# Where the last heads are normalised and split, and when the squares of w1 and w3 are issued, in a fused attention and gated feed-forward kernel

## The chip, the cores and the metric

The kernel runs on one core of a Trainium2 chip. Its engines are TensorE (PE in the profile, with its weight loads as PEld), VectorE (DVE), ScalarE (ACT), GpSimd (POOL) and SyncE (SP), which here only issues transfers between on-chip memory (SBUF) and DRAM. Each engine works off its own queue in order and waits in that queue for what its next instruction needs. The metric is the time of one execution on the device, in microseconds.

## The reference

For x of 2048 tokens by 512 channels:

```python
xn = _layernorm(x)
s = attention(xn, wqkv, wo)        # 32 heads of 16, causal, window of 256 keys, scale 1/4
g = _silu(((_silu(xn @ w1) * (xn @ w3)) @ w2))     # 512 -> 1792 -> 512
return x + s * g
```

In the attention, scores outside the window are set to -1e9 before the softmax. wqkv, wo, w1, w2 and w3 are drawn at run time and multiplied by 8, so the kernel has to find their magnitude itself.

## The kernel before

**Numbers.** Every matrix product but the scores' mask and the values is done in 16-bit pieces: an operand is scaled by a power of two and split into a high part (its cast to fp16) and a low part (what the cast left out), and three products are summed: high by high, high by low, low by high. A split is two instructions, a cast and a subtraction. It is done by ScalarE and GpSimd (the helper `halves`, line 340, runs an elementwise operation on two halves of 256 columns; all its users appear under L340) or by ScalarE and VectorE.

**Tiling.** The tokens are worked through in four tiles t of 512. In each, the 32 heads make four groups g of eight, and a group two units p of four heads; there are 16 pairs (t, g) and 32 units. Attention takes two passes over the scores of a unit. `pass1` computes them to find each row's maximum on VectorE (L662, L676); `pass2` computes them again with the keys on the partitions (L742), adds the masks (L749, VectorE), takes the exponential (L752, ScalarE) and multiplies by the values (L770). The values carry a column of ones, so the denominators come out of the same matmuls.

**From heads to the operand of the output projection.** When a unit's values are done, `finish` (inside `pass2`) moves them to SBUF (`os`), to the tile `on` of the group (eight heads by 16 channels on 128 partitions, 512 tokens) and the denominators to a DRAM tile `dd`. After the second unit, `normalise(t, g)` runs:

- it loads the denominators as a 128 by 32 tile `dr` (L807);
- `invert`, 12 steps later: reciprocal (L812) and scale (L813) on VectorE, a store to the DRAM tile `de` (L815), eight broadcasting loads into `rb` (L819), and on GpSimd the product of `on` and `rb` in two halves (L340). The VectorE part stands inside `issue_after(lasts["emptied"])`, which ties it behind the latest instruction that emptied a PSUM bank;
- `cut`, 26 steps later: GpSimd casts `on` to the high part (L826, two halves) and subtracts for the low part (L340, two halves). The result `O[t, g]` is an operand of `total`.

A step is one piece of work of the program that is written next; `later(n, f)` runs f after n more of them.

**Feed-forward.** `gate_up` (L1013) multiplies by w1 and w3, and L1028, L1032, L1037 and L1046 form and split the product of silu and up; `down` (L1238) multiplies by w2. From t = 2 on the down projection is folded: seven products instead of eight (L1156), whose banks are emptied by L1174, and which `unfold` (L1190) adds up, on VectorE in the last tile. `total` then takes tanh of the result (L1284, ScalarE; a tie to the last exponential stands there too), finishes the silu (L1285), runs the output projection (L1290, 12 matmuls for each of the row blocks b), evicts (L1294), adds x (L1296) and stores. For the last tile this runs for b = 1, 3, 0, and `total_by_columns` does b = 2 in two halves of 256 columns (L1312 to L1323).

**Weights in the first tile.** w1, w3 and w2 are loaded in float32 during t = 0 only (L849 for w1 and w3), measured, split and stored to DRAM in fp16 for the later tiles. To measure means: the sum of squares of each piece (`squares`), a cast of the sums (L262), a matmul with ones that adds them over the partitions (L281 or L286), and a chain of small VectorE instructions that makes a power of two (`powers`). `squares` puts the first `on_act` pieces on ScalarE (L250) and the others on VectorE (L252). `measure(f)` asks for four pieces, two of them on ScalarE for f = 0 and 2, all four afterwards; the weights of q, k and v use `squares` too, with two on ScalarE. Squares of w2 have an instruction of their own in `measure_down`.

**What sets the order.** TensorE's order is the order in which the program is written. The queues of the other engines and of SyncE are put in order by a scheduler that goes by priorities (`urgent` raises one) and by operands, and that obeys `issue_after`: the instruction is put behind the named one in its queue. `behind_exp()` is such a tie, to the latest exponential (L752) issued so far, if there is one.

PSUM, where matmuls write, has two banks m0 and m1 that `bank` hands out in turn to all dense products, two pairs of banks for scores and one pair (po) for the values.

Of the kernel before, what the change touches and what calls it, by code (L numbers as in the profile page):

```python
# [14 lines left out]
AF = mybir.ActivationFunctionType  # L15
# [68 lines left out]
def tile_block(ctx: ExitStack, tc: tile.TileContext, x, wqkv, wo, w1, w3, w2, out):  # L84
    nc = tc.nc
# [27 lines left out]
    def take(dtype):  # L113
        free.sort()
        slot = free.pop(0)[2]
        made = fpool.tile([P, 512 if dtype == F32 else 1024], dtype, name=slot, tag=slot, bufs=1)
        held[id(made)] = slot, made
        return made
# [25 lines left out]
    def later(n, f):  # L144
        made_so_far[0] += 1
        queue.append((now[0] + n, made_so_far[0], f))
# [85 lines left out]
    def behind_exp():  # L232

        return tc.issue_after(lasts["exp"].ins) if "exp" in lasts else nullcontext()
# [5 lines left out]
    def squares(parts, on_act=0, apart=0):  # L240


        ssq = small.tile([P, len(parts)], F32, name="ssq")

        def one(i, raw):

            sq = ppool.tile([P, D], BF16, name="sqa" if i < on_act else "junk", bufs=1)
            if i < on_act:
                with behind_exp():
                    nc.scalar.activation(sq, raw, AF.Square, accum_out=ssq[:, i:i + 1])  # L250
            else:
                nc.vector.tensor_tensor_reduce(out=sq, in0=raw, in1=raw, scale=1.0, scalar=0.0,  # L252
                                               op0=ALU.mult, op1=ALU.add, accum_out=ssq[:, i:i + 1])
        for i, raw in enumerate(parts):
            if apart:
                later(apart * (i + 1), lambda i=i, raw=raw: one(i, raw))
            else:
                one(i, raw)
        sb = small.tile([P, len(parts)], BF16, name="sb")

        def cast():
            lasts["cast"] = nc.vector.tensor_copy(sb, ssq)  # L262
        def behind_bank():

            with tc.issue_after(lasts["emptied"].ins) if "emptied" in lasts else nullcontext():
                cast()
        if apart:
            later(apart * (len(parts) + 1) + 1, behind_bank)
        else:
            cast()  # L270
        return sb
# [65 lines left out]
    def halves(op, out, a, b):  # L337

        for c in (slice(0, 256), slice(256, 512)):
            op(out[:, c], a[:, c], b[:, c])  # L340
# [81 lines left out]
    lasts = {}  # L422
# [298 lines left out]
    def pass2(t, g, p):  # L721
# [54 lines left out]
        def finish():  # L776
            os = opool.tile([P, TW], F32, name="os", bufs=1)
            po = cell["po"]

            def rest():  # L780

                c = slice(0 if t else 64, TW)

                with urgent(), tc.issue_after(lasts["emptied"].ins):
                    nc.vector.tensor_copy(os, po[:, 0, :])
                    nc.vector.tensor_add(os[:, c], os[:, c], po[:, 1, c])
                if p == 0:
                    ON[t, g] = (opool.tile([P, TW], F32, name="on", bufs=1), dpool.tile([8, TW], F32, name="dd"))
                on, dd = ON[t, g]
                for i in range(4):  # L790
                    h = (i // 2) * 4 + 2 * p + i % 2
                    nc.sync.dma_start(on[16 * h:16 * h + 16, :], os[32 * i:32 * i + 16, :])
                nc.sync.dma_start(dd[4 * p:4 * p + 4, :], os[DH::32, :])
                if p == 1:
                    normalise(t, g)
            later(1, rest)
# [6 lines left out]

    def normalise(t, g):
        on, dd = ON.pop((t, g))
        dr = small.tile([P, 32], F32, name="dr")
        nc.sync.dma_start(dr, dd.rearrange("h (b c) -> (h b) c", c=32))  # L807
        rb = opool.tile([P, TW], F32, name="rb", bufs=1)

        def invert():  # L810
            with tc.issue_after(lasts["emptied"].ins):
                nc.vector.reciprocal(dr, dr)  # L812
                nc.vector.tensor_scalar(dr, dr, sc["o"], None, op0=ALU.mult)  # L813
            de = dpool.tile([8, TW], F32, name="de")
            nc.sync.dma_start(de.rearrange("h (b c) -> (h b) c", c=32), dr)  # L815
            for i in range(8):
                p, r, a = i // 4, i // 2 % 2, i % 2
                h = r * 4 + 2 * p + a
                nc.sync.dma_start(rb[16 * h:16 * h + 16, :], de[i:i + 1, :].to_broadcast([16, TW]))  # L819
            halves(nc.gpsimd.tensor_mul, on, on, rb)  # L820

        def cut():
            OT[t, g] = made = take(F16)
            O[t, g] = o = made.rearrange("p (a q) -> p a q", a=2)
            for c in (slice(0, 256), slice(256, 512)):
                nc.gpsimd.tensor_copy(o[:, 0, c], on[:, c])  # L826
            halves(nc.gpsimd.tensor_sub, o[:, 1, :], on, o[:, 0, :])
        later(12, invert)
        later(26, cut)

# [553 lines left out]
    tiles = [(t, g) for t in range(NT) for g in range(NG)]  # L1386
# [190 lines left out]
    for n in range(len(units)):  # L1577
        t = n // 8
# [69 lines left out]
```

## Time and profile before

| | us |
|---|---|
| median of 3 runs | 824.89 |
| lowest and highest of them | 822.91, 829.77 |
| the profiled execution, whole | 824.23 |
| its span in the trace | 822.3 |
| VectorE, ScalarE, GpSimd busy in the span | 632.8, 393.9, 374.3 |

The span runs from the first recorded instruction to the last; the profiled execution's own time has 1.9 us around it. All times in the trace count from the span's start. PE is TensorE, PEld its weight loads, DVE VectorE, ACT ScalarE, POOL GpSimd, SPq, DVEq and so on the engines' sequencers. A line such as L340 is a line of the kernel before; rows name the operation as out<-in with the program's tile names, where `slot` is any of the 55 tiles that are reused for everything without a name of its own, m a bank of the dense products and s a pair of banks of scores.

Three views are used in the prediction. In the page's groups and in the waits, a row gives busy time, count and the idle time ahead, with what ended it. In the chain of waits a row is a start time, a duration and what was on the path then; "issue" is time without any visible wait. In the timeline a row is a start time, how long the row's instructions took together, the engine, line, operation and shapes, the count (x), and in square brackets the idle time just ahead and what ended it. A window row gives start and end, length, the busy time and instruction count of PE, PEld, DVE, ACT and POOL, the granted TensorE clock as a share of full speed, the share of DMA engines busy and GB/s.

### The profile page before, as it was taken

What the parts mean: (1) busy time and instruction counts of PE and PEld (TensorE: products, weight loads), DVE (VectorE), ACT (ScalarE), POOL (GpSimd) and SP (SyncE); (2) the same over time, 40 slices, a digit from 0 to 9 for tenths busy, and PEclk for the clock granted to TensorE, in tenths of its full rate; (3) what the DMA queues carried; (4) which work ended last, traced back from release to release, by engine and by line L of the source; (5) the groups of instructions that cost most, each with busy time, mean ns of one, the idle gap of its engine ahead of it and who ended that gap; (6) DMA issues with size and microseconds to landing.
All of it is one profiled execution on the core that took longest, in us unless ns stands there. A gap on an engine that the chain in (4) does not pass through costs nothing.

```text
span 822.3 us, 23929 instructions
## 1 busy us (share of the span) xinstructions
PE 797.6 (97%) x9176; PEld 404.8 (49%) x9176; DVE 632.8 (77%) x2032; ACT 393.9 (48%) x594; POOL 374.3 (46%) x660
## 2 busy tenths in 40 slices
PE   8997989999999999999999999999999999999995
PEld 4433444444445444444445444466545744466472
DVE  8787688788888767887988887777677877874454
ACT  6879576563546544344443444344444243444410
POOL 2236366232329447155262546330446374831833
PEclk9999999999999999999999999999999999999998
DMA  9979664665743486747555453745543662244311
GB/s 283 256 239 301 220 204 151 209 201 151 211 138 92 144 251 197 215 123 219 159 147 173 122 154 89 203 139 165 171 119 107 169 195 70 62 140 143 123 47 53
DMA packets 109923, 134.71 MB, mean 164 GB/s; under 512 B 18736, under 2 KB 64752, under 8 KB 109808
## 3 DMA queue, kind: packets, MB, share of 16 engines
q1 hardware_dynamic: 109520, 132.66, 54.6%
q8 instruction: 72, 1.18, 0.6%
q10 hardware_dynamic: 288, 0.52, 0.2%
q14 instruction: 43, 0.35, 0.1%
HBM read 91.75 MB, written 37.09 MB: 157 GB/s over the span
## 4 chain that ended last, share of the span: by engine, by line
PE 73%; DVE 10%; DMA 5%; POOL 3%; issue 3%; ACT 3%; SPq 2%; DVEq 0%; POOLq 0%; ACTq 0%
PE m L1013 27%; PE po L770 8%; PE m L1156 7%; PE m L1238 6%; PE m L594 6%; PE s L742 5%; PE m L1290 4%; PE m L564 4%; DVE junk L676 3%; PE s L662 2%; POOL slot L340 2%; DMA slot<-in_B_w_dram 2%; PE po L662 1%; DVE s L749 1%; PE m L1508 1%
## 5 line engine op out<-in xcount | busy, mean ns | idle before, releaser
L1013 PE MATMUL m<-XH,slot 128*128 128x512 f16 x896 | 267.3, 380 | 2.3 <-DVE slot L615 1.0
L752 ACT ACTIVATE pt<-s,es 128x1024 f32<-128x1024 f32 x152 | 167.5, 1112 | 191.1 <-DVE s L749 185.1
L340 POOL TENSOR_TENSOR slot<-slot,slot 128x256 f16<-128x256 f32 (+1 forms) x178 | 117.7, 689 | 204.3 <-ACT slot L1046 80.8
L1013 PEld LDWEIGHTS <-slot 128*128 128x128 f16 x1344 | 124.8, 98 | 156.7 <-issue 13.2
L1013 PE MATMUL m<-XL,slot 128*128 128x512 f16 x448 | 169.8, 379 | 0.0
L749 DVE TENSOR_TENSOR s<-s,MK 128x256 f32<-128x256 f32 (+2 forms) x280 | 118.8, 435 | 52.5 <-PE s L742 47.9
L676 DVE CUSTOM_DVE_ANT_0 junk<-s,MW 128x320 bf16<-128x320 f32 x276 | 134.0, 485 | 17.5 <-PE s L662 11.0
L676 DVE CUSTOM_DVE_ANT_0 junk<-po,MW 128x320 bf16<-128x320 f32 x172 | 83.5, 485 | 4.3
L1238 PE MATMUL m<-slot,slot 128*128 128x512 f16 x336 | 79.2, 380 | 2.5 <-POOL slot L340 2.1
L770 PE MATMUL po<-pt,V 64*32 64x320 f32 (+4 forms) x2880 | 77.2, 342 | 0.7 <-DVE pp L305 0.7
L594 PE MATMUL m<-XH,slot 128*128 128x512 f16 x240 | 70.9, 380 | 1.5 <-DVE slot L1032 0.7
L1156 PE MATMUL m<-slot,slot 128*128 128x256 f16 x588 | 68.4, 273 | 0.0
L1071 POOL TENSOR_TENSOR slot<-slot,slot 128x256 f16<-128x256 f32 x98 | 64.6, 670 | 1.2
L1028 ACT ACTIVATE slot<-m,sgs 128x512 f32<-128x512 f32 x56 | 38.2, 683 | 55.6 <-PE m L1013 50.3
L1156 PEld LDWEIGHTS <-slot 128*128 128x128 f16 x588 | 56.2, 98 | 11.4 <-issue 2.8
L770 PEld LDWEIGHTS po<-pt,V 64*32 64x32 f32 x2880 | 50.5, 106 | 22.8 <-issue 0.8
L1032 DVE SCALAR_TENSOR_TENSOR slot<-slot,m 128x512 f32<-128x512 f32 x56 | 38.3, 684 | 28.1 <-ACT slot L1028 28.1
L742 PE MATMUL s<-qa,KA 50*64 50x320 f16 (+3 forms) x1472 | 58.4, 259 | 0.2 <-DMA qa<-dm 0.2
L594 PEld LDWEIGHTS <-slot 128*128 128x128 f16 x384 | 35.7, 98 | 44.6 <-issue 3.2
L340 POOL TENSOR_TENSOR on<-on,rb 128x256 f32<-128x256 f32 x32 | 26.3, 842 | 64.9 <-DMA rb<-de 42.6
L742 PEld LDWEIGHTS <-KA 50*64 50x64 f16 x1472 | 30.2, 105 | 52.0 <-issue 29.9
L1238 PEld LDWEIGHTS <-slot 128*128 128x128 f16 x336 | 30.7, 98 | 41.4 <-issue 7.5
(186 smaller groups left out, 1125.2 us busy)
## 6 DMA issues: line engine op xcount, KB each, us to landing
slot<-dW SPq DMA_DIRECT2D x98, 256.0 KB
slot<-in_B_w_dram SPq DMA_DIRECT2D x56, 256.0 KB
slot<-dFold SPq DMA_DIRECT2D x48, 256.0 KB
dW<-slot SPq DMA_DIRECT2D x42, 256.0 KB
slot<-in_A_x_dram SPq DMA_DIRECT2D x30, 256.0 KB
KA<-dK SPq DMA_DIRECT2D x24, 288.0 KB
qa<-dQ SPq DMA_DIRECT2D x32, 192.0 KB
slot<-dWQ SPq DMA_DIRECT2D x24, 256.0 KB
```

The source lines that it names most:

```text
L340: op(out[:, c], a[:, c], b[:, c])
L594: nc.tensor.matmul(cell["pp"], w[:, (a * NC + c) * P:(a * NC + c + 1) * P], b[:, c, :], start=(c, i) == parts[0][0], stop=(c, i) == parts[ ...
L676: lasts["maximum"] = nc.vector.tensor_tensor_reduce(out=junk[:, :n], in0=s[:, r, :n], in1=mask, scale=1.0, scalar=NEG, op0=ALU.add, op1=AL ...
L742: nc.tensor.matmul(s[64 * h:64 * h + 64, r, o:o + 64 * n], ka[rows, 2 * p + a, 64 * (m + 4):64 * (m + 5)], qa[rows, 2 * p + a, 64 * (m + k ...
L749: nc.vector.tensor_add(v, v, MK[:, kind, of:of + n, :].unsqueeze(1).to_broadcast([P, 2 * len(which), n, 64]))
L752: lasts["exp"] = nc.scalar.activation(pt, s, AF.Exp, scale=es)
L770: nc.tensor.matmul(cell["po"][32 * i:32 * i + 32, h, 64 * (m + k):64 * (m + k + n)], V[64 * h:64 * h + 64, (4 * t + m // 2) % VB, hd * VW: ...
L1013: nc.tensor.matmul(cell[k], w[:, (a * NC + c) * P:(a * NC + c + 1) * P], b[:, c, :], start=c == 0 and i == 0, stop=c == NC - 1 and i == 2)
L1032: lasts["emptied"] = nc.vector.scalar_tensor_tensor(sg, sg, 1.0, cell[0], op0=ALU.add, op1=ALU.mult)
L1071: nc.gpsimd.tensor_sub(lo, view, hi)
L1156: nc.tensor.matmul(cell["ps"][:, c], made[:, f:f + P], wj[:, g:g + 256], start=j == j0 and c == 0 and n == 0, stop=j == j1 - 1 and n == 2, ...
L1238: nc.tensor.matmul(ps, hh[:, a * TW + b * P:a * TW + (b + 1) * P], w[:, c * D:(c + 1) * D], start=f == f0 and i == 0, stop=f == f1 - 1 and ...
```

## The change

Three edits. In `squares`, the squares on ScalarE are no longer tied behind the latest exponential; operands, shapes and number of instructions stay. In `normalise`, for the last pair (t, g) alone: `invert` runs 6 steps later instead of 12 and its VectorE part is not tied behind the emptying of a bank; and `cut` runs 12 steps later instead of 26 and makes the high part by one copy of 128 by 512 on ScalarE and the low part by one subtraction on VectorE, instead of four half-size instructions on GpSimd. The product of `on` and `rb` stays on GpSimd. In the built program TensorE's order is the same in both kernels; on VectorE the reciprocal and the scale (L812, L813) stand behind the second of seven L1174 of the last fold instead of behind the fourth, and the new subtraction stands between the last two L1190; on ScalarE the new copy stands between the second and the third of the last L1284, and squares of w1 and w3 stand earlier among the work of t = 0.

```diff
--- before.py
+++ after.py
@@ -246,8 +246,7 @@
 
             sq = ppool.tile([P, D], BF16, name="sqa" if i < on_act else "junk", bufs=1)
             if i < on_act:
-                with behind_exp():
-                    nc.scalar.activation(sq, raw, AF.Square, accum_out=ssq[:, i:i + 1])
+                nc.scalar.activation(sq, raw, AF.Square, accum_out=ssq[:, i:i + 1])
             else:
                 nc.vector.tensor_tensor_reduce(out=sq, in0=raw, in1=raw, scale=1.0, scalar=0.0,
                                                op0=ALU.mult, op1=ALU.add, accum_out=ssq[:, i:i + 1])
@@ -803,12 +802,13 @@
 
     def normalise(t, g):
         on, dd = ON.pop((t, g))
+        last = (t, g) == tiles[-1]
         dr = small.tile([P, 32], F32, name="dr")
         nc.sync.dma_start(dr, dd.rearrange("h (b c) -> (h b) c", c=32))
         rb = opool.tile([P, TW], F32, name="rb", bufs=1)
 
         def invert():
-            with tc.issue_after(lasts["emptied"].ins):
+            with nullcontext() if last else tc.issue_after(lasts["emptied"].ins):
                 nc.vector.reciprocal(dr, dr)
                 nc.vector.tensor_scalar(dr, dr, sc["o"], None, op0=ALU.mult)
             de = dpool.tile([8, TW], F32, name="de")
@@ -822,11 +822,15 @@
         def cut():
             OT[t, g] = made = take(F16)
             O[t, g] = o = made.rearrange("p (a q) -> p a q", a=2)
+            if last:
+                nc.scalar.copy(o[:, 0, :], on)
+                nc.vector.tensor_sub(o[:, 1, :], on, o[:, 0, :])
+                return
             for c in (slice(0, 256), slice(256, 512)):
                 nc.gpsimd.tensor_copy(o[:, 0, c], on[:, c])
             halves(nc.gpsimd.tensor_sub, o[:, 1, :], on, o[:, 0, :])
-        later(12, invert)
-        later(26, cut)
+        later(6 if last else 12, invert)
+        later(12 if last else 26, cut)
 
 
 
```

## Prediction

> **What bounds the kernel now.** I read the page first, then TensorE's waits, then the chain of waits for the last 30 us, and last the engines' timelines there and around 60 us.
>
> ```profile
> span 822.3 us, 23929 instructions
> PE 797.6 (97%) x9176; PEld 404.8 (49%) x9176; DVE 632.8 (77%) x2032; ACT 393.9 (48%) x594; POOL 374.3 (46%) x660
> ...
> PE m L1290 <- POOL slot L826: 5.1, 1, 5.1
> PE m L1238 <- POOL slot L340: 2.1, 3, 1.0
> PE s L286 <- DVE sb L262: 2.0, 1, 2.0
> ```
>
> TensorE is busy 97% of the span, and neither kernel's TensorE order differs from the other's, so a gain can only be an idle gap that closes or a clock that stays up. The largest gap is one wait of 5.1 us: the output projection (L1290) waits for the split of the last heads (L826). The next two belong to the squares' side of the change: L286 waits for a cast (L262) of the sums of squares, L1238 for GpSimd's splits. The chain shows what lies before the large one:
>
> ```profile
> 795.73 1.39 DMA de<-dr
> ...
> 797.14 0.32 SPq L819
> ...
> 800.28 1.78 DMA rb<-de
> ...
> 802.22 4.00 issue
> 806.22 0.72 POOL on L340
> ...
> 807.33 8.51 PE m L1290 x27
> 815.84 2.63 PE m L1319 x24
> ...
> 819.02 0.42 DVE slot L1322
> ```
>
> The inverted denominators go to DRAM (1.39 us), come back in eight broadcasts, and land at 800.28 + 1.78 = 802.06. Then GpSimd multiplies, casts and subtracts, and TensorE goes on at 807.33.
>
> **The inversion is moved forward.** It stood behind the fourth L1174 and now stands behind the second.
>
> ```profile
> 747.18 0.38 SPq L807 DMA_DIRECT2D dr<-dd  x1
> 749.86 0.35 DVE L812 RECIPROCAL dr<-dr 128x32 f32<-128x32 f32 x1 [1.30 <-DMA dr<-dd]
> ...
> 788.29 0.38 SPq L807 DMA_DIRECT2D dr<-dd  x1
> 790.57 0.75 DVE L1174 SCALAR_TENSOR_TENSOR slot<-m,fd,slot 128x512 f32<-128x512 f32 x1 [1.29 <-PE m L1156]
> 795.09 0.34 DVE L812 RECIPROCAL dr<-dr 128x32 f32<-128x32 f32 x1
> ```
>
> Its operand dr is fetched at 788.29 in both kernels. For the heads before these, VectorE sat idle for dr and began 749.86 - 747.18 = 2.68 us after the issue, so dr is there at about 790.97. The second L1174 ends at 790.57 + 0.75 = 791.32, and small operations begin just under such an end: the reciprocal starts at 791.25 instead of 795.09, 3.84 us sooner. SyncE has only this chain left then, so the store and the eight L819 move by as much, and the broadcasts land at 798.2; with the 0.12 us that GpSimd took from landing to start, its multiply could start at 798.34. If dr came 1 us late, the third L1174 would stand behind a waiting reciprocal; it has about 1 us of idle time ahead of it, so that costs nothing here.
>
> **The multiply meets VectorE.** This is the disputed term.
>
> ```profile
> 758.96 1.41 POOL L340 TENSOR_TENSOR on<-on,rb 128x256 f32<-128x256 f32 x2
> 802.18 4.75 POOL L340 TENSOR_TENSOR on<-on,rb 128x256 f32<-128x256 f32 x2 [8.36 <-DMA rb<-de]
> ...
> 797.17 1.43 DVE L340 TENSOR_TENSOR slot<-slot,slot 128x256 f32<-128x256 f32 x4
> 798.51 0.42 DVE L1190 TENSOR_TENSOR slot<-slot,slot 128x256 f32<-128x256 f32 x1
> 798.85 0.74 DVE L1174 SCALAR_TENSOR_TENSOR slot<-m,fd,slot 128x512 f32<-128x512 f32 x1
> 799.51 1.42 DVE L1190 TENSOR_TENSOR slot<-slot,slot 128x256 f32<-128x256 f32 x4
> 800.85 0.74 DVE L1174 SCALAR_TENSOR_TENSOR slot<-m,fd,slot 128x512 f32<-128x512 f32 x1
> ...
> 802.51 0.75 DVE L1190 TENSOR_TENSOR slot<-slot,slot 128x256 f32<-128x256 f32 x2
> ...
> 804.99 0.68 DVE L1313 SCALAR_TENSOR_TENSOR slot<-slot,slot 128x512 f32<-128x512 f32 x1
> ```
>
> The same two halves took 1.41 us earlier and 4.75 us here: the first could not end until 806.22, 0.55 us after VectorE's unbroken run of operations with two SBUF inputs ended at 804.99 + 0.68 = 805.67. Now the multiply arrives at 798.34, inside such a run, which lasts to 798.51 + 0.42 = 798.93; then comes an L1174, one of whose inputs is a PSUM bank (m). I take it that the first half passes under it, ending at 798.93 + 0.55 = 799.5. The second half either follows at once (ends 800.2, and VectorE's four adds slip 0.65 us) or waits for these adds and passes under the next L1174 (ends 800.93 + 0.55 = 801.5). I take the second.
>
> The Trainium skill, page "SBUF — State Buffer", section "Who interferes with whom", says that a VectorE instruction with two SBUF inputs and a GpSimd instruction that reads SBUF exclude each other for a whole instruction, whoever starts first. By that rule the trace agrees on who collides, but not on how long: the multiply stood through eight VectorE instructions, not one. Read by the single instruction, both halves would be done by about 800.0 and the sum would be that of the first variant.
>
> **The split moves to ScalarE and VectorE.**
>
> ```profile
> 800.35 1.15 ACT L1284 ACTIVATE slot<-slot 128x512 f32<-128x512 f32 x2 [12.35 <-PE m L1156]
> ...
> L344 ACT CAST slot<-slot 128x512 f16<-128x512 f32 x46 | 27.0, 611 | 0.1
> ...
> 807.58 1.29 POOL L340 TENSOR_TENSOR slot<-on,slot 128x256 f16<-128x256 f32 x2
> ...
> 809.74 0.69 DVE L1296 TENSOR_TENSOR slot<-slot,slot 128x512 f32<-128x512 f32 x1
> ```
>
> ScalarE's copy is queued behind two L1284, which end at 801.50; a 128x512 cast costs 0.61, so the high part is there at 802.15. VectorE's subtraction is queued behind the first of the last two L1190 (802.93) and costs 0.69: the low part is there at 803.6 (804.2 in the variant where VectorE slips). Before, half of the low part was there at 807.58 + 0.65 = 808.23. So TensorE passes its last stall 4.7 us sooner (4.1). New waits: VectorE now waits inside its queue for the copy, with an L1190, three L1285 and the evictions L1294 behind it. The first eviction then ends near 805.8; its bank is wanted by the third projection, at about 803.6 + 13 x 0.22 = 806.4, so it is covered by 0.6 us, and would cost what it exceeds that. GpSimd loses two casts and two subtractions, with nothing behind them.
>
> **The clock.**
>
> ```profile
> 800.11 2.10 PE L1290 MATMUL m<-slot,slot 128*128 128x512 f16 x9
> ...
> 60.00:80.00 20.00, 16.77 (x142) 7.30 (x140) 15.30 (x65) 18.24 (x36) 11.97 (x19) 1.00 0.96 295
> 807.30:812.40 5.10, 5.07 (x12) 1.63 (x13) 1.44 (x2) 0.00 (x0) 1.57 (x3) 0.51 0.14 53
> ```
>
> After the 5.1 us of idleness TensorE's granted clock was 0.51 for 5.1 us. The gap now is about 1 us of waiting for the low part; the 2.0 us wait for L262 lies inside 60 to 80 us, where the granted clock was 1.00. So I expect full clock: from the low part on, 25 matmuls of 0.215 to 0.233 us (nine took 2.10) end at 809.0 to 809.4, against 815.84: 6.4 to 6.8 us, less 0.6 in the slipped variant. Kept at half, the clock would take back about 2.2 (8.51 against 27 x 0.233). The Trainium skill, page "TensorE: Matmul & The Clock Gate", section "Part 1: The HAM clock gate (the "warmup" mystery)", gives half rate after one idle window of some 3.4 us; the 5.1 us row agrees. What follows (L1319, its evictions, the stores) is unchanged. I take 6.5 for the tail.
>
> **The squares.** Bytes and instructions stay; their places in ScalarE's queue move.
>
> ```profile
> 58.50 0.62 ACT L1046 CAST slot<-slot 128x512 f16<-128x512 f32 x1 [1.37 <-DVE slot L1037]
> 66.17 0.62 ACT L250 ACTIVATE sqa<-slot 128x512 bf16<-128x512 f32 x1
> 67.86 0.63 ACT L250 ACTIVATE sqa<-slot 128x512 bf16<-128x512 f32 x1
> ...
> 38.35 2.95 SPq L849 DMA_DIRECT2D slot<-in_B_w_dram  x4
> 60.47 6.86 DMA slot<-in_B_w_dram
> ...
> DVE sb L262 <- ACT sqa L250: 5.0, 4, 2.6
> ```
>
> Two squares go from 66.17 and 67.86 into ScalarE's idle 1.37 us ahead of 58.50. Their operands are loaded by the four L849 issued until 38.35 + 2.95 = 41.30; with the slowest landing of the chain (6.86) they are there by 48.2, nine before they are read. ScalarE was busy 18.24 of the 20 us from 60 to 80, and splits and squares that TensorE waits for sit in that run; it gets 0.62 + 0.63 = 1.25 us shorter, so the 2.0 us wait for L262 shrinks to 0.75 and the GpSimd splits come as much sooner. At the other groups (near 97, 122 and 146 us) squares also move up; each is worth between -1 (L262 now stands ahead of two mask additions and may hold them) and +1.25. I take 1.25 in all, bounds -1 and +3.75.
>
> **The sum.** The profiled execution took 824.23, 1.9 over its span and 0.66 under the median shown (824.89): 824.23 - 6.5 - 1.25 = 816.5.
>
> **Rivals.** (a) The squares give more: two more groups pay 1.25 each, 814.0. For: VectorE lost 5.0 us to L262 in all. (b) Their gain is given back before 200 us, because VectorE, not ScalarE, ends the waits there: 817.8. For: VectorE's 77% are denser than ScalarE's. (c) The multiply is shut out until VectorE itself stops at its wait for the copy, 802.93; for it speaks the 4 us stall above, against it that no operation with a PSUM input lay in that run. High part at 804.9, low part at 805.7, 2.1 later: 818.6; if that longer gap also halves the clock, which decides between 2.0 and 5.1 us of idleness, 820.8. (d) The change does not do what it says, because dr lands only with the fourth L1174: about 823. (e) Slower than before: untied squares stand in ScalarE's in-order queue ahead of L1046 and L1028, which free TensorE's banks; a square whose load is late holds both, TensorE with them. It decides from 7.75 us of holding; at 10 us the time is 826.5. Against: the nine spare us.
>
> **Chances.** Forecast 0.55 (815 to 818 by its variants), (a) 0.10, (b) 0.14, (c) 0.10 and 0.04 with the clock, (d) 0.02, (e) 0.05. A measurement here tells about 1% from no change, 8.2 us, so from 816.6 down; my forecast stands on that edge. Faster: half of the forecast, all of (a), a little of (b): 0.42. Slower by over 1% needs 16 us of (e): 0.03. Same: 0.55. The range 813.5 to 820.0 holds the forecast, (a), (b) and (c) without the clock.
>
> **What would show it.** The reciprocal near 791.3 by the old clock (less the front's shift) and the multiply's first half ending under an L1174: step one right. A multiply of over 2 us with VectorE adds beside it: (c). A granted clock of 1.00 up to the last matmul: the clock's term. L286's wait under 1 us: the squares. I am wrong if TensorE's last stall is still over 3 us, or if new ScalarE waits on loads stand before 150 us.

## The result, and the profile after

The changed kernel takes 818.38 us (median of 6 runs, 817.41 to 820.43), the kernel before 825.35 us beside it (6 runs); the ratio is 0.9914 with a 95% interval of 0.9886 to 0.9941, so 4.9 to 9.4 us less, about 7.1. The ratio is taken over all the executions and is not that of the two medians. In a later series it took 819.27 us against 826.79, ratio 0.9908 (0.9878 to 0.9938). One slow execution of the kernel before, of 1606.63 us beside the last run below, is left out everywhere. The forecast was 816.5 us in a range of 813.5 to 820.0, or 7.75 us under the profiled execution of before. The profiled execution after has a span of 816.1 us against 822.3, 6.2 less.

The page's head after, and TensorE's waits after (us in total, times, longest):

```profile
span 816.1 us, 23926 instructions
PE 796.3 (98%) x9176; PEld 404.3 (50%) x9176; DVE 633.0 (78%) x2033; ACT 395.1 (48%) x595; POOL 371.0 (45%) x656
```

```profile
PE m L1242 <- POOL slot L339: 2.1, 3, 1.0
...
PE s L285 <- DVE sb L261: 1.1, 2, 0.9
...
PE m L1294 <- DVE slot L827: 0.8, 1, 0.8
```

Lines after L249 are shifted: L1294 is the output projection (L1290 before), L1242 the down projection (L1238), L1178 the eviction of the fold (L1174), L1194 the unfold (L1190), L339 the halves (L340), L826 and L827 the new copy and subtraction. The 5.1 us wait of the last projection is now 0.8 us, and the 2.0 us wait for the sums of squares is 0.9.

The timeline of the tail after:

```profile
792.28 0.35 DVE L812 RECIPROCAL dr<-dr 128x32 f32<-128x32 f32 x1 [0.22 <-DMA dr<-dd]
...
799.41 2.86 POOL L339 TENSOR_TENSOR on<-on,rb 128x256 f32<-128x256 f32 x2 [4.83 <-DMA rb<-de]
799.60 0.74 DVE L1178 SCALAR_TENSOR_TENSOR slot<-m,fd,slot 128x512 f32<-128x512 f32 x1
800.26 1.42 DVE L1194 TENSOR_TENSOR slot<-slot,slot 128x256 f32<-128x256 f32 x4
800.86 2.72 PE L1294 MATMUL m<-slot,slot 128*128 128x512 f16 x11
...
801.60 0.74 DVE L1178 SCALAR_TENSOR_TENSOR slot<-m,fd,slot 128x512 f32<-128x512 f32 x1
...
802.30 0.62 ACT L826 CAST slot<-on 128x512 f16<-128x512 f32 x1
...
803.60 0.68 DVE L827 TENSOR_TENSOR slot<-on,slot 128x512 f16<-128x512 f32 x1
...
804.34 5.57 PE L1294 MATMUL m<-slot,slot 128*128 128x512 f16 x25 [0.76 <-DVE slot L827]
...
809.74 2.78 PE L1323 MATMUL m<-slot,slot 128*128 128x256 f16 x24
```

The two halves of GpSimd's product, looked at one by one, ran from 799.41 to 800.27 and from 800.23 to 802.27: each ends under one of the two L1178, whose input m is a PSUM bank; the second was held through the four L1194 between them. Copy and subtraction follow, TensorE waits 0.76 us, and 25 matmuls take 5.57 us, 0.22 each: full clock.

A measure of the tail that does not depend on what came before: from the first matmul of the output projection to the end of the last matmul. Before, that is 800.11 to 815.84 + 2.63, or 18.36 us; after, 800.86 to 809.74 + 2.78, or 11.66: 6.7 us less. The start of that stretch is 0.75 us later than before, though, so the front as a whole gave nothing in this execution.

Where the front's gain went is seen in the timeline of TensorE at the first down projections, before and after:

```profile
76.32 1.03 PE L1238 MATMUL m<-slot,slot 128*128 128x512 f16 x4
...
81.81 2.53 PE L1238 MATMUL m<-slot,slot 128*128 128x512 f16 x11 [0.87 <-POOL slot L340]
```

```profile
74.46 1.03 PE L1242 MATMUL m<-slot,slot 128*128 128x512 f16 x4
...
78.28 0.81 PE L1242 MATMUL m<-slot,slot 128*128 128x512 f16 x3 [0.98 <-POOL slot L339]
79.96 4.22 PE L1242 MATMUL m<-slot,slot 128*128 128x512 f16 x11 [0.87 <-POOL slot L339]
```

The first four are 1.86 us earlier. The last eleven begin 1.85 us earlier too, but take 4.22 us instead of 2.53, so they end 0.16 us ahead. The windows say why (columns: stretch, length, busy time and count of PE, PEld, DVE, ACT and POOL, granted clock, DMA share, GB/s); before, then after:

```profile
80.00:84.00 4.00, 2.99 (x14) 1.29 (x14) 2.65 (x10) 3.79 (x7) 3.09 (x6) 1.00 1.11 342
```

```profile
80.00:84.00 4.00, 4.00 (x11) 1.47 (x11) 1.16 (x3) 4.00 (x9) 4.00 (x7) 0.57 1.08 371
```

Behind two waits of 0.98 and 0.87 us the granted clock, the mean over this stretch, was 0.57 of full speed. The remaining 0.9 us of the front's loss lies scattered between 84 and 800 us; the six runs of the changed kernel have spans of 815.6 to 818.7 us, so a profile is not read to that amount.

### The profile page after: what moved, and what is told of

Its sections match the earlier page's. It is cut to its first block, busy times and chain, and to the rows that moved or that the text cites. A ratio compares the mean times of both kernels' runs of the same rounds, so it can differ in the third digit from the quotient of the medians.

```text
span 816.1 us, 23926 instructions
## 1 busy us (share of the span) xinstructions
PE 796.3 (98%) x9176; PEld 404.3 (50%) x9176; DVE 633.0 (78%) x2033; ACT 395.1 (48%) x595; POOL 371.0 (45%) x656
## 4 chain that ended last, share of the span: by engine, by line
PE 71%; DVE 13%; ACT 6%; DMA 4%; issue 3%; POOL 2%; SPq 0%; DVEq 0%; POOLq 0%; ACTq 0%
PE m L1017 27%; PE m L1242 8%; PE po L769 7%; PE m L1160 7%; PE m L593 6%; PE s L741 5%; DVE junk L675 4%; PE m L1294 3%; PE m L563 3%; PE s L661 2%; DVE s L748 2%; PE po L661 1%; ACT slot L342 1%; ACT pt L751 1%; ACT slot L343 1%
## 5 line engine op out<-in xcount | busy, mean ns | idle before, releaser
L339 POOL TENSOR_TENSOR slot<-slot,slot 128x256 f16<-128x256 f32 (+1 forms) x178 | 117.8, 691 | 207.1 <-ACT slot L1050 77.9
L1242 PE MATMUL m<-slot,slot 128*128 128x512 f16 x336 | 80.9, 386 | 2.5 <-POOL slot L339 2.1
L339 POOL TENSOR_TENSOR on<-on,rb 128x256 f32<-128x256 f32 x32 | 24.4, 785 | 61.3 <-DMA rb<-de 48.1
L1242 PEld LDWEIGHTS <-slot 128*128 128x128 f16 x336 | 31.1, 99 | 42.6 <-issue 9.8
```

Source lines behind the costliest of these rows:

```text
L1242: nc.tensor.matmul(ps, hh[:, a * TW + b * P:a * TW + (b + 1) * P], w[:, c * D:(c + 1) * D], start=f == f0 and i == 0, stop=f == f1 - 1 and ...
```

## The experiments

The tail column is the measure above in us, from the run's one trace; times are medians in us. The tail of the kernel before is 18.4.

| run | time, before beside it | ratio (95%) | tail |
|---|---|---|---|
| the change | 818.38, 825.35 | 0.9914 (0.9886 to 0.9941) | 11.7 |
| squares alone | 824.71, 826.63 | 0.9968 (0.9943 to 0.9993) | 17.5 |
| tail alone | 820.70, 826.63 | 0.9927 (0.9906 to 0.9948) | 12.7 |
| early inversion alone | 822.31, 826.63 | 0.9964 (0.9937 to 0.9991) | 12.2 |
| split's engines alone | 826.76, 826.63 | 0.9993 (0.9971 to 1.0015) | 18.1 |
| gap filled | 823.67, 826.21 | 0.9980 (0.9953 to 1.0007) | 16.4 |
| no GpSimd in the last heads | 823.11, 826.21 | 0.9968 (0.9943 to 0.9992) | 15.3 |
| the change again | 819.27, 826.79 | 0.9908 (0.9878 to 0.9938) | 11.7 |
| change, split in halves | 818.38, 826.79 | 0.9894 (0.9866 to 0.9923) | 11.1 |
| change, split on GpSimd | 821.86, 826.79 | 0.9938 (0.9917 to 0.9960) | 15.0 |
| change, two squares on VectorE | 820.23, 826.79 | 0.9910 (0.9877 to 0.9942) | 14.4 |
| both last edits | 817.00, 825.67 | 0.9890 (0.9866 to 0.9915) | 11.1 |

**Squares alone.** The kernel before with this edit:

```diff
-                with behind_exp():
-                    nc.scalar.activation(sq, raw, AF.Square, ...)
+                nc.scalar.activation(sq, raw, AF.Square, ...)
```

> The kernel before with the squares of w1 and w3 untied and nothing else. Theory: the wait of L286 near 71 us falls from 2.0 to about 0.9 us, but by 83 us TensorE is no more than 0.5 us ahead of the kernel before, because it then waits for splits that ScalarE and GpSimd deliver no sooner, and at times runs a stretch of about 3 us at half clock behind these waits; the tail keeps its 5.1 us stall. Whole time: 0 to 1 us under before. Rival (my forecast): the 1.25 us stay, the time is 1.0 to 1.5 us under before and TensorE is as far ahead at 90 us and at 780 us. Other rival: later groups pay too, 2 us or more under before.

In the trace the theory fell and my forecast's size held. The wait near 71 us is 0.85 us, the waits behind it are those of the changed kernel, but the clock stayed up:

```profile
78.75 0.81 PE L1237 MATMUL m<-slot,slot 128*128 128x512 f16 x3 [0.98 <-POOL slot L339]
80.42 4.48 PE L1237 MATMUL m<-slot,slot 128*128 128x512 f16 x20 [0.87 <-POOL slot L339]
```

20 matmuls in 4.48 us is full speed, and they begin 81.81 - 80.42 = 1.39 us sooner than before; at the first output projection the lead is still 800.11 - 799.02 = 1.09 us. The span is 2.2 us shorter, 820.1 against 822.3, but not by the squares alone: behind the same stall of 5.1 us the 27 matmuls of the tail took 7.66 us instead of 8.51. The time, 0.6 to 4.7 us under before, does not separate the three readings. So the half clock is not a sure consequence of these waits; the same two waits are followed by it in one execution and not in the other.

**Tail alone.** The change without the edit to the squares.

> The kernel before with the change in the last heads' normalisation and split alone. Theory: this is the whole gain: the last TensorE stall falls from 5.1 to 0.8 us, the clock stays at 1.00 behind it, 6 to 7.3 us under before, the same as the changed kernel within 1 us. Rival: the front's part carries 1.25 us or more of the 7, so this run is 5.3 to 6 us under before.

0.9927: 4.3 to 7.8 us, most of the change, and with the squares alone (0.6 to 4.7) the parts add up to the whole within their intervals. The median, 5.9 us under before, lies with the rival, but the interval holds the theory too. The tail of its trace, though, took another course than in the changed kernel:

```profile
799.93 0.74 DVE L1179 SCALAR_TENSOR_TENSOR slot<-m,fd,slot 128x512 f32<-128x512 f32 x1
800.52 1.59 POOL L340 TENSOR_TENSOR on<-on,rb 128x256 f32<-128x256 f32 x2 [5.61 <-DMA rb<-de]
800.59 2.47 DVE L1195 TENSOR_TENSOR slot<-slot,slot 128x256 f32<-128x256 f32 x4
...
804.19 0.60 PE L1295 MATMUL m<-slot,slot 128*128 128x512 f16 x2 [0.90 <-ACT slot L827]
...
805.73 5.57 PE L1295 MATMUL m<-slot,slot 128*128 128x512 f16 x25 [0.93 <-DVE slot L828]
```

The product began in the second half of the PSUM eviction (799.93 to 800.67) instead of ahead of it, so it was still running when VectorE wanted its first add. Now GpSimd's halves took 1.59 us and VectorE's four adds 2.47 instead of 1.42 us: it was VectorE that waited. TensorE's last waits are 0.90 and 0.93 us, the tail is 1.06 us longer.

The front of this trace is that of the kernel before, and shows something else. Behind the old wait for the sums of squares the clock fell:

```profile
73.25 0.20 PE L286 MATMUL s<-sb,onesb 64*64 64x4 bf16 x4 [1.99 <-DVE sb L262]
```

```profile
73.76:77.17 3.41, 3.41 (x9) 1.21 (x8) 2.92 (x13) 3.41 (x6) 2.86 (x5) 0.50 0.69 156
```

The same happens behind this wait in the split's engines alone, the gap filled and the run without GpSimd, but neither in the kernel before nor in the early inversion alone. It costs little there, because TensorE waits for splits soon after: the 0.87 us wait ended at 81.81 in the kernel before, the 1.00 us wait in its place ended at 82.00 here.

**Early inversion alone**, the split left on GpSimd:

```diff
+        last = (t, g) == tiles[-1]
...
-            with tc.issue_after(lasts["emptied"].ins):
+            with nullcontext() if last else tc.issue_after(lasts["emptied"].ins):
...
-        later(12, invert)
-        later(26, cut)
+        later(6 if last else 12, invert)
+        later(12 if last else 26, cut)
```

> The kernel before with the last inversion early and its split programmed earlier, but the split left on GpSimd. Theory: the multiply passes under two L1174 as in the changed kernel (done by about 802 us), then GpSimd's casts and subtractions meet VectorE's unbroken run of operations with two SBUF inputs and the first half of the low part is there only some 0.5 us after that run ends, near 806 us: the stall stays above 3.5 us, the clock behind it falls to about half, and the time is 1.5 to 3.5 us under before. Rival: GpSimd is not shut out by such a run once it has begun, the low part's first half is there at about 803 us, and this run gains as much as the whole change, 6 us or more.

```profile
801.08 0.74 DVE L1175 SCALAR_TENSOR_TENSOR slot<-m,fd,slot 128x512 f32<-128x512 f32 x1
801.49 1.59 POOL L340 TENSOR_TENSOR on<-on,rb 128x256 f32<-128x256 f32 x2 [5.43 <-DMA rb<-de]
801.74 2.70 DVE L1191 TENSOR_TENSOR slot<-slot,slot 128x256 f32<-128x256 f32 x4
...
803.03 1.13 POOL L827 CAST slot<-on 128x256 f16<-128x256 f32 x2
...
804.13 1.47 POOL L340 TENSOR_TENSOR slot<-on,slot 128x256 f16<-128x256 f32 x2
```

In the trace the theory fell: GpSimd came in during an eviction again, and from there its casts and subtractions took turns with VectorE's adds. The price is on VectorE, whose eviction then holds the third projection for 1.13 us. The time, by the ratio about 3 us under before (0.7 to 5.2), fits the theory and is less than that trace's tail (6.2 us shorter) would give; the run with the split on GpSimd, below, shows another course that would explain it, but how often each comes is not known from one trace.

**Split's engines alone**, the inversion where it was:

```diff
+            if last:
+                nc.scalar.copy(o[:, 0, :], on)
+                nc.vector.tensor_sub(o[:, 1, :], on, o[:, 0, :])
+                return
```

> The kernel before with the split of the last heads on ScalarE and VectorE, but the inversion where it was. Theory: the multiply is shut out as before until about 806.9 us, then 0.62 us of copy and 0.69 us of subtraction put the low part at about 808.2 us, where its first half was before: within 0.7 us of before, the stall about 5 us, the clock behind it half. Rival: the split's engine is what counts (one whole copy and subtraction are quicker than four instructions of GpSimd, and VectorE's queue is shorter), 2 us or more under before.

```profile
805.29 4.75 POOL L340 TENSOR_TENSOR on<-on,rb 128x256 f32<-128x256 f32 x2 [8.36 <-DMA rb<-de]
...
810.74 7.97 PE L1295 MATMUL m<-slot,slot 128*128 128x512 f16 x27 [5.43 <-ACT slot L827]
```

As the theory had it: the product takes its 4.75 us whoever splits, and the tail is within 0.3 us of before. The time agrees; by its interval at most 2.4 us could be gained.

**Change, split on GpSimd**: the early inversion alone with the untied squares.

> The changed kernel with the split of the last heads left on GpSimd (untied squares, early inversion, earlier split, all four split instructions on GpSimd). Theory now: GpSimd, once it is in first, holds VectorE back instead of being shut out, the low part comes as early, and VectorE's later evictions cost about 0.5 us: within 1.3 us of the changed kernel. Rival (the first forecast for the early inversion): the split is shut out, 3 us or more over the changed kernel.

```profile
799.79 2.90 POOL L339 TENSOR_TENSOR on<-on,rb 128x256 f32<-128x256 f32 x2 [4.80 <-DMA rb<-de]
802.63 3.60 POOL L826 CAST slot<-on 128x256 f16<-128x256 f32 x2
806.20 1.29 POOL L339 TENSOR_TENSOR slot<-on,slot 128x256 f16<-128x256 f32 x2
```

```profile
805.95 7.76 PE L1290 MATMUL m<-slot,slot 128*128 128x512 f16 x27 [2.57 <-POOL slot L826]
```

In the trace the theory I had by then fell and the first one came back: the tail is 3.4 us longer than the changed kernel's. The time, 2.6 us over by the medians, points the same way, though the two ratios' intervals overlap. Here the product came in ahead of the eviction, as in the changed kernel; the first cast, recorded 0.05 us ahead of VectorE's run of adds and silu products (802.68 to 805.63), was held through it and took 3.26 us; TensorE waited 2.57 us and went on at half clock. So both courses exist with the same edit of the inversion. In all eight traces with the early inversion the start of the product goes with the course: 0.11 to 0.24 us ahead of the eviction in five, and its second half is held for over a microsecond; 0.41 to 0.59 us inside the eviction in three, and VectorE waits about 1 us. That the landing of rb decides it is argued from this, not tried. The changed kernel takes the split off GpSimd, so no cast of GpSimd can be held for 3 us: its tail is 11.7 us against 15.0 in the first course, and 12.7 against 12.2 in the second, where the split on GpSimd is no worse.

**No GpSimd in the last heads**, the inversion late; the split is written 13 steps later instead of 26, and the silu product of the last row block has the same tie as the one shown last:

```diff
-            halves(nc.gpsimd.tensor_mul, on, on, rb)
+            if not last:
+                halves(nc.gpsimd.tensor_mul, on, on, rb)
...
+            if last:
+                nc.vector.tensor_mul(on, on, rb)
+                nc.scalar.copy(o[:, 0, :], on)
+                lasts["low"] = nc.vector.tensor_sub(o[:, 1, :], on, o[:, 0, :])
+                return
...
+                with tc.issue_after(lasts["low"].ins) if t == NT - 1 else nullcontext():
+                    nc.vector.scalar_tensor_tensor(y, y, 1.0, acc, op0=ALU.add, op1=ALU.mult)
```

> The kernel before with the inversion where it was, but no GpSimd in the last heads: the product with the inverted denominators and the subtraction are one VectorE operation each, ahead of the last silu products, and the copy is on ScalarE. Theory: the broadcasts land at about 802 us as before, VectorE multiplies at 803.2 to 803.9, ScalarE copies until 804.8 and the low part is there at 805.5 instead of 808.2: the shut-out multiply alone cost 2.7 us of the tail, with up to 2.3 us more if the shorter stall (about 2.6 us and 0.5 us) leaves the clock up; 2.5 to 5 us under before. Rival: the landing of the broadcasts sets the end, not the meeting of GpSimd and VectorE: under 1.5 us.

```profile
806.40 7.98 PE L1298 MATMUL m<-slot,slot 128*128 128x512 f16 x27 [2.54 <-ACT slot L829]
```

```profile
808.00:811.30 3.30, 3.30 (x9) 1.19 (x8) 2.74 (x5) 0.00 (x0) 0.00 (x0) 0.50 0.11 38
```

3.1 us off the tail with the broadcasts as late as before. TensorE's stall, 2.54 us instead of 5.12, is 2.6 of it, as the theory had it; the other 0.5 is the 27 matmuls behind it, 7.98 us instead of 8.51. So keeping the two engines apart is worth about 2.6 us by itself, though VectorE's one product of 512 columns stands for GpSimd's two halves here. The time, 0.7 to 4.7 us under before, agrees. Half clock followed a wait of 2.54 us too.

**Gap filled.** The kernel before with idle work in the 5.1 us:

```diff
             for g in (2 * half, 2 * half + 1):
+                if g == NG - 1 and (t, b) == (NT - 1, 1):
+                    spare = scores_bank()[:, 0, :].rearrange("p (a b) -> p a b", a=4)
+                    for _ in range(20):
+                        nc.tensor.matmul(spare, onesb, onesb.unsqueeze(1).to_broadcast([P, 4, P]), ...)
```

> The kernel before with 20 matmuls of ones (128x512, into a spare bank, their result is not used) put between the ninth and the tenth matmul of the last tile's first output projection, where TensorE waits 5.1 us. They last about 4.3 us, so the stall is filled to 0.8 us and everything else stays. Theory: only the clock behind the stall changes, to 1.00, and the matmuls from the split to L1319 take about 2.2 to 2.6 us less: the time is 2.2 to 2.6 us under before. Rival: the half clock comes from something else than the idleness (it stays 0.5), or what follows is bound by VectorE, and the time is that of before within 0.7 us.

```profile
805.21 4.48 PE L1292 MATMUL s<-onesb 128*128 128x512 bf16 x20
810.50 0.61 PE L1294 MATMUL m<-slot,slot 128*128 128x512 f16 x2 [0.81 <-POOL slot L826]
811.48 5.57 PE L1294 MATMUL m<-slot,slot 128*128 128x512 f16 x25 [0.37 <-POOL slot L340]
```

GpSimd's stall is as before (4.06 us for the first half), and 25 matmuls take 5.57 us. From the restart to the last matmul it is 9.2 us instead of 11.1 (807.33 to 818.47): the clock's share of that tail is 2.0 us, a little under the theory. It is not the same in every execution: in the squares alone, behind the same stall of 5.12 us, this stretch takes 10.3 us (806.24 to 816.52), 1.1 over the filled one. The time itself leaves it open (0.9980, 0.9953 to 1.0007).

**The change again.**

> The changed kernel once more, beside the next three on the same chip. 6 to 8 us under before. If the half clock near 80 us in its profile is a matter of where the waits fall in the chip's own time, it is there in some executions and absent in others with the same waits; if it follows from the waits of the changed kernel, it is there again whenever they are.

The half clock near 80 us was there, as in the profile of the split in halves; in the squares alone and the split on GpSimd it was absent with the same two waits. Of the change's first six runs three have a mean clock of 1.000 and three of 0.998, and one stretch of 3.41 us at half clock lowers the mean over 816 us by 0.002. So the changed kernel itself has it in some executions and not in others. The first reading is the right one; the last section shows from the traces what the fall goes with.

**Change, split in halves**:

```diff
-                nc.scalar.copy(o[:, 0, :], on)
-                nc.vector.tensor_sub(o[:, 1, :], on, o[:, 0, :])
+                for c in (slice(0, 256), slice(256, 512)):
+                    nc.scalar.copy(o[:, 0, c], on[:, c])
+                    nc.vector.tensor_sub(o[:, 1, c], on[:, c], o[:, 0, c])
```

> The changed kernel with ScalarE's copy and VectorE's subtraction in two halves of 256 tokens. The next row block needs the first half alone. Theory: the first half of the low part is there at about 0.4 to 0.6 us sooner than the whole one, the last stall falls from 0.8 to about 0.2 us and the time by about 0.5 us, less than can be told from no change in the time. Rival: VectorE's evictions, now later by what the second instruction costs, hold the third projection instead, and nothing is gained.

The last wait is 0.34 us and the tail 0.56 us shorter, as expected; the time (818.38 against 819.27) agrees and can't tell it from nothing.

**Change, two squares on VectorE**:

```diff
-        sb = squares([...], on_act=4 if f > 2 else 2, apart=apart)
+        sb = squares([...], on_act=2 if f in (0, 2, 6) else 4, apart=apart)
```

> The changed kernel with two of the four squares that TensorE waits for near 71 us on VectorE instead of ScalarE. Theory: ScalarE is what ends the waits between 60 and 86 us, so the wait of L285 (0.85 us) goes, the splits that GpSimd waits for come up to 1.6 us sooner, and TensorE is 1.2 to 2.5 us ahead of the changed kernel at 90 us and stays so. Rival: the squares (0.77 us each) stand in VectorE's queue ahead of masks and maxima and take the same time away there: TensorE is ahead by less than 0.5 us at 90 us.

The front did most of what the theory said: no wait near 71 us, though a new one of 1.02 us at 68.91, behind VectorE, and matmuls near 115 us 3.1 us ahead of the changed kernel, 1.7 of them the half clock that isn't there. The whole time did not move. In its trace the lead was gone by 432 us, where the scores waited for the maxima (first line) and half clock followed, and the tail fell to the other course with half clock (the others):

```profile
427.46 0.51 PE L741 MATMUL s<-qa,KA 50*64 50x256 f16 x8 [2.70 <-DMA qa<-dm]
...
805.02 0.60 PE L1294 MATMUL m<-slot,slot 128*128 128x512 f16 x2 [0.89 <-ACT slot L826]
806.55 1.31 PE L1294 MATMUL m<-slot,slot 128*128 128x512 f16 x4 [0.93 <-DVE slot L827]
```

```profile
807.00:810.50 3.50, 3.50 (x10) 1.27 (x9) 2.90 (x5) 0.55 (x1) 0.00 (x0) 0.53 0.02 5
```

These waits are those of the tail alone within 0.01 us, where the windows over the same stretch show the clock up:

```profile
807.00:810.50 3.50, 3.50 (x18) 1.58 (x17) 3.50 (x7) 0.00 (x0) 0.00 (x0) 1.00 0.18 64
```

**Both last edits**, the split in halves and the two squares on VectorE, on the changed kernel:

> The changed kernel with both last edits: copy and subtraction in halves, and two of the squares on VectorE. Theory: no half clock near 80 us (no wait of TensorE over 1.1 us is left there), TensorE 2 us or more ahead of the changed kernel near 115 us, and a tail of 11.1 to 12.2 us from the first output projection's first matmul to the last matmul; 8.5 to 10.5 us under before. Rival: what is gained before 240 us goes again into later waits for transfers of the maxima (near 425 us), whose landing does not move, and the time is that of the changed kernel, 7 to 8 us under before.

817.00 us, 8.7 under the kernel before beside it: the lower end of the theory, but the ratio's interval, 7.0 to 11.1 us, holds the rival's 7 to 8 too. Its mean clock was 0.999 or 1.000 in every run, its tail 11.1 us. A part of the rival holds too: 1.0 us of wait for the maxima near 425 us. Against the changed kernel's 0.9908 and 0.9914, its 0.9890 is a gain of 1.5 to 2 us that the intervals don't separate.

## Why the prediction was right, step by step

All times here are on the new clock; the forecast's are moved by the 0.75 us by which the last stretch began later.

- *The reciprocal*: forecast 792.0, measured 792.28, held 0.22 us by dr: it began 3.24 us after the issue of dr's load (789.04) and not 2.68.
- *The multiply*: the disputed term, right in its course. The first half was to end at 800.25 and did at 800.27, the second at 802.25 and did at 802.27. That this variant came was close and in part luck: the product began 0.19 us ahead of the eviction (799.41 and 799.60), and in three of the eight traces with the early inversion it began inside it. The variant in which VectorE slips exists too; I gave it 0.65 us, and it costs 1.05. Rival (c), the multiply shut out until VectorE's own wait, did not occur in any trace with the early inversion.
- *The split*: copy done at 802.92 (forecast 802.90), subtraction at 804.28 (804.35). The forecast's 4.7 us is what the low part gained against the start of the projection: 8.14 us behind it before (808.25), 3.42 after. But neither edit is half of it: the split's engines alone gave nothing, and the early inversion with the split on GpSimd gave 3.3 us of the tail in one trace and 6.2 in another.
- *The clock*: full up to the last matmul, worth 2.0 us by the filled gap against the profiled execution of before, where I had 2.2, and 1.1 against the trace of the squares alone. Tail in all: 6.7 us, forecast 6.5.
- *The squares*: two of them went into ScalarE's hole as forecast, ahead of the cast that had waited there:

```profile
56.53 0.63 ACT L249 ACTIVATE sqa<-slot 128x512 bf16<-128x512 f32 x1
...
57.28 0.63 ACT L249 ACTIVATE sqa<-slot 128x512 bf16<-128x512 f32 x1
...
57.91 0.60 ACT L1050 CAST slot<-slot 128x512 f16<-128x512 f32 x1
```

That cast stood at 58.50 before, so this execution was 0.6 us ahead by then; ScalarE's order up to there is the same in both, and the squares alone were only 0.13 ahead (58.37), so I put it down to other reasons. TensorE's wait shrank to 0.85 us (forecast 0.75), and the splits came as much sooner, as the forecast had it: TensorE is 1.85 us ahead at 79.96, 1.26 of them since that cast. What failed is that these 1.25 us were carried to the end ("I take 1.25 in all"): the three waits for GpSimd's splits are 2.1 us in all in both kernels, but the two long ones now stand closer together, and behind them the same eleven matmuls took 1.7 us longer. What is left of the squares is 1.4 us when the clock stays up, as in the squares alone, and next to nothing when it falls.
- *The clock again*: I took a wait of 2.0 us as safe and priced half clock only for longer ones, from one execution. That premise was wrong: behind this very wait the clock fell to 0.50 in four of the six traces that kept it, and it followed two waits of 0.9 us in others. The full clock of the tail came true with a single wait of 0.76 us, for which TensorE still worked 2.96 us of the 3.41 us period (803.89 to 807.30; the last section says what the periods are). The profiled execution gained 6.3 us (824.23 to 817.94) where the sum had 7.75: the tail gave 0.2 more, what follows the last matmul 0.3, and the front 2.0 less, -0.75 instead of 1.25 (0.6 from other causes and 1.25 from the squares, less 1.7 for the clock and the scattered 0.9). So the tail's term held. The squares' term did not, in this execution; that its bound of -1 us covered what the clock took is luck, for the bound was there for mask additions held by L262.
- *The measurement*: I took 8.2 us as the least that it can tell from no change. It told about 7.1, with an interval of 4.9 to 9.4.

## What to carry to other kernels

An operation of GpSimd that reads SBUF late in a kernel is not priced by its duration but by what VectorE runs at that moment: look for the instructions of VectorE with a PSUM operand, and ask whether the operation arrives before or after they begin. Taking what follows it off GpSimd was worth nothing alone and 3.4 us of the tail in one course of the earlier input, so test such edits apart and together, and more than once. Time taken from one in-order queue is given to whatever the scheduler pulls forward: follow the instruction that the bottleneck waits for, not the sum. And a clock that falls behind the same waits in one execution and not in the next makes a gain of 1 to 2 us come and go: look at more than one trace before calling a wait safe.

## What the runs showed of the hardware

VectorE and GpSimd exclude each other in both directions here: one GpSimd multiply of 0.72 us took 4.07 behind VectorE's unbroken run, and two adds of VectorE took 0.94 us each instead of 0.42 when GpSimd had begun first. The Trainium skill, page "SBUF — State Buffer", section "Who interferes with whom", says that the order of issue decides who blocks; the multiply of the kernel before agrees, and adds that the second in line may stand through a whole unbroken run, eight instructions of VectorE, and not only through one. Where two starts are recorded within 0.05 us of each other the traces don't tell the order: the product's second half after (800.23, VectorE's add 800.26) and the cast in the split on GpSimd (802.63, the add 802.68) are recorded just ahead and were held all the same.

TensorE's granted clock fell to 0.5 for 3.41 or 6.83 us at a time: behind waits of 2.5 us and more in the tail, and behind shorter ones in some executions and not in others. The traces show what this goes with. In each of the thirteen, every change of the clock lies a whole number of 3.41 us after the first rise, and that first rise comes anywhere from 3.86 to 6.78 us of the span. Cut into these periods, a trace shows how busy TensorE was in each. Here are the tail alone and the two squares on VectorE, which have the same two waits of 0.9 us:

```profile
800.80:804.21 3.41, 2.52 (x16) 1.15 (x14) 3.41 (x7) 1.66 (x3) 1.31 (x2) 1.00 0.00 0
804.21:807.62 3.41, 2.48 (x11) 0.99 (x12) 3.41 (x8) 1.26 (x2) 0.00 (x0) 1.00 0.00 0
```

```profile
803.77:807.18 3.41, 1.60 (x7) 0.42 (x6) 3.41 (x9) 2.08 (x5) 0.00 (x0) 1.00 0.01 2
807.18:810.59 3.41, 3.41 (x9) 1.18 (x8) 2.72 (x5) 0.37 (x1) 0.00 (x0) 0.50 0.02 5
```

In the first the two waits fall into two periods, in the second into one, and behind that one the clock is 0.50. Near 80 us it is the same: TensorE was busy 1.56 us of the period with both waits in the changed kernel, but 2.15 and 2.54 in the squares alone, where a period ends between the waits. Over all the traces every fall follows a period with 1.62 us or less of work, and no period with 1.68 or more is followed by one; one period with 1.62 is not (before, 71.63 to 75.04). So what counts here is the idle time within one period, about half of it, and where the periods lie decides between two executions with the same waits. This is read from the traces, with modelled ends of the matmuls; no run was made to try it. The same skill's page "TensorE: Matmul & The Clock Gate", section "Part 1: The HAM clock gate (the "warmup" mystery)", has the low clock after an idle window of some 3.4 us; these rows show it after periods in which TensorE still worked for up to 1.6 us.
